# Attention in front of a mixture of experts: Q is loaded into 64 partitions instead of twice into 128

## The chip, the cores and the metric

The kernel runs on one core of one Trainium2 chip. The metric is the device time of one execution in microseconds (us), lower is better. Five engines work side by side, each on its own instruction queue: TensorE (PE, its weight loads are listed apart as PEld), VectorE (DVE), ScalarE (ACT), GpSimd (POOL) and SyncE (SP), which here only issues DMAs. A DMA is issued by a queue and then carried out by the core's 16 DMA engines. SBUF is the on-chip memory with 128 partitions; PSUM is what TensorE writes to.

## What is computed

Three layers follow each other. Only the first is touched by the change.

```python
# 1. attention: 4 batches x 8 heads, S = 576 rows, head size 64
scores = scale * np.matmul(q, k.transpose(0, 1, 3, 2))
s_pos = np.maximum(s, 0.0)
cum = np.cumsum(s_pos, axis=-1)
bias = -(cum[:, :, :, None] - cum[:, :, None, :])
scores = np.where(causal, -1000000000.0, scores + np.minimum(bias, 0.0))
attn = softmax(scores)             # max, exp, sum, divide
x = np.matmul(attn, v)             # then rows of 8 heads side by side: 2304 x 512
# 2. experts: 8 experts of 288 tokens each, tokens assigned greedily by logit
h = np.maximum(x[mask] @ w1[e], 0.0); out[mask] = h @ w2[e]
# 3. a dense layer: relu(x @ w_in) squared, @ w_out
```

## The kernel before

All matrix products are made in a 4-byte matmul type, `fp32r`. To keep full precision a float32 operand is split in two: a high part (the operand rounded to `fp32r`) and a low part (the operand less its high part). A product of two such operands then takes the terms high·high, low·high and high·low.

The attention uses the head size of 64 for this. For a head, `Q1` holds in its partitions 0 to 63 the high part of Q (transposed, so that the head dimension lies on the partitions) and in its partitions 64 to 127 the low part. `K1` holds the high part of K in both halves. One matmul of `Q1` with `K1` over all 128 partitions therefore gives high·high + low·high. `Q2` holds the high part of Q again (64 partitions) and four rows for the bias, `K2` the low part of K and four rows for the bias; a second matmul of `Q2` with `K2` over 68 partitions gives the rest.

The 32 heads are worked in 16 pairs. `load_pair(p)` loads Q and K of a pair from HBM into `q2` and `k2`, each of 128 partitions and 2 heads of 576 columns, by two DMAs each: the same 64 rows go to partitions 0 to 63 and again to 64 to 127. `prep(head, u)` makes the parts of a head. For every pair but the first, u = 0 rounds `q2` into `Q1` on DVE (L179) and copies the high part from `Q1` to `Q2` by a DMA on SP's queue (L180); u = 1 rounds `k2` into `K1` on DVE (L182), and POOL subtracts twice: K's low part into `K2` (L183) and Q's low part into the upper half of `Q1` (L184). For the first pair ACT rounds Q (L160) and writes `Q2` (L161), and DVE makes Q's low part (L177).

Each head has five score tiles, i = 4 down to 0. Each tile goes through two matmuls (L225 and L226), a mask, a row maximum on DVE (L248), an exponential on ACT (L260), transposes on TensorE (L282), copies out of PSUM on DVE or ACT, and products with V (L312). The tile i = 0 of the two heads of a pair is one tile: its two matmuls (L210) read `Q1` and then `Q2` of both heads, and they stand among the tiles of the pair's first head. The order is written out by hand: the program counts tiles, ten to a pair, and at tile numbers given by `PR` and `PR0` calls `prep` for the heads of the next pair, at tile 5 of each pair `load_pair` for the pair after that. So the second head of a pair is prepared at tile 9 of the pair before, and its `Q2` is read at tile 4 of its own pair.

SP issues nearly all DMAs in program order: the copy of the first head's `Q2`, the loads of K and Q, in most pairs one or two blocks of the third layer's weights (L912, `r<-in_wout`, 512 KB each), the copy of the second head's `Q2`, the loads of V and four or five small copies of bias rows.

After attention come the assignment of tokens to experts, the experts, and the dense layer; TensorE carries these.

Of the kernel before, what the change touches and what calls it, by code (L numbers as in the profile page):

```python
# [6 lines left out]
FT = mybir.dt.float32  # L7
# [4 lines left out]
AF = mybir.ActivationFunctionType  # L12
OP = mybir.AluOpType
# [3 lines left out]
B, H, S, D = 4, 8, 576, 64  # L17
# [16 lines left out]
def f32(ap):  # L34
    return ap.bitcast(FT)
# [33 lines left out]
def attention(tc, cn, qT, kT, vm, vt, s, wg, xd, L):  # L69
    nc = tc.nc  # L70
# [3 lines left out]
    def pool(name, bufs, **kw):  # L74
        p = tc.tile_pool(name=name, bufs=bufs, **kw)
        pools.append(p)
        return p.__enter__()
# [6 lines left out]
    ld = pool("a_ld", 2)  # L84
# [7 lines left out]
    RAW = {}  # L92

    def load_pair(p):
        q2 = ld.tile([128, 2, S], FT, name="q2")
        k2 = ld.tile([128, 2, S], FT, name="k2")
        if p == 0:
            todo = ((nc.scalar, q2, qT, 0, 1), (nc.sync, k2, kT, 0, 1), (nc.sync, k2, kT, 1, 2),
                    (nc.sync, q2, qT, 1, 2))
        else:  # L100
            todo = ((nc.sync, k2, kT, 0, 2), (nc.sync, q2, qT, 0, 2))
        for eng, t, src, a0, a1 in todo:
            if p == 1 and t is q2:
                bias(1)

            h = src[:, 2 * p + a0:2 * p + a1, :]
            for r in (0, 64):
                eng.dma_start(t[r:r + 64, a0:a1], h)
        RAW[p] = (q2, k2)

# [5 lines left out]
    def load_v(p):  # L116
# [4 lines left out]
        VB[p] = t  # L121

    load_pair(0)
    QB = fx.tile([128, 2, S], FR, name="QB")
    Q2S = [QB[0:68], fx.tile([68, 2, S], FR, name="Q21")]
    K2S = [fx.tile([68, 2, S], FR, name=f"K2{k}") for k in range(2)]

    def ones(k):
        for n, t in enumerate((Q2S[k], K2S[k])):
            nc.scalar.activation(t[64:68], cn.one[64:68, n:n + 1, None].to_broadcast([4, 2, S]), AF.Copy)  # L130
# [10 lines left out]
    PREP = {}  # L141

    def bias(hd):
        p, a = hd // 2, hd % 2
        r = f32(brow[hd:hd + 1])
        nc.sync.dma_start(f32(K2S[p % 2][66:68, a]), r)
        t = f32(Q2S[p % 2][64:66, a])
        if a:
            nc.sync.dma_start(t, r)
        else:  # L150

            nc.sync.dma_start(t[:, :S - 64], r[:, :, 64:])
            nc.sync.dma_start(t[:, S - 64:], r[:, :, :64])

    def prep0():
        q2 = RAW[0][0]
        PREP[0] = (wk.tile([128, 2, S], FR, name="Q1"), wk.tile([128, 2, S], FR, name="K1"), Q2S[0], K2S[0])
        bias(0)
        for a in range(2):
            nc.scalar.activation(PREP[0][0][:, a], q2[:, a], AF.Copy)  # L160
            nc.scalar.activation(Q2S[0][0:64, a], q2[0:64, a], AF.Copy)  # L161
        ones(1)
        prep(0, 0)

    def prep(hd, u):
        p, a = hd // 2, hd % 2
        q2, k2 = RAW[p]
        if p not in PREP:
            PREP[p] = (wk.tile([128, 2, S], FR, name="Q1"), wk.tile([128, 2, S], FR, name="K1"), Q2S[p % 2],
                       K2S[p % 2])  # L170
        Q1, K1, Q2, K2 = (t[:, a] for t in PREP[p])
        q, k = q2[:, a], k2[:, a]
        if u == 0:
            if p == 0:
                nc.vector.tensor_copy(K1, k)
                (nc.gpsimd if a else nc.vector).tensor_tensor(K2[0:64], k[0:64], f32(K1[0:64]), op=OP.subtract)
                nc.vector.tensor_tensor(Q1[64:128], q[64:128], f32(Q1[64:128]), op=OP.subtract)  # L177
                return
            nc.vector.tensor_copy(Q1, q)  # L179
            nc.sync.dma_start(f32(Q2[0:64]), f32(Q1[0:64]))  # L180
        else:
            nc.vector.tensor_copy(K1, k)  # L182
            nc.gpsimd.tensor_tensor(K2[0:64], k[0:64], f32(K1[0:64]), op=OP.subtract)  # L183
            nc.gpsimd.tensor_tensor(Q1[64:128], q[64:128], f32(Q1[64:128]), op=OP.subtract)  # L184
            if a:
                RAW.pop(p)

# [218 lines left out]
    def run_jobs(n):  # L406
        for _ in range(n):
            if jobs:
                f, a = jobs.popleft()
                f(*a)  # L410

    prep0()
    for k in range(2):
        nc.vector.memset(sums[k], 1.0)
    load_pair(1)
    load_v(0)
    cn.late_consts(0)
# [26 lines left out]
    AVO = [1, 8]  # L444
    at(2, tri_of_two)
    at(A1, prep, 1, 0)
    at(A1, RAW.pop, 0)
    at(26, gate_weights)
    for n in range(4):
        at(15 + n, cn.late_consts, 1 + n)  # L450
    for p in range(NP):
        t0 = 10 * (p + 1) + LA
        last = p == NP - 1
        avs, avo = (LS_, LO_) if last else (AVS, AVO)
        for n in range(7):
            at(t0 + avs[n], av, p, n)
        at(t0 + avo[0], av_out, p, 0)
        at(t0 + avo[1], av_out, p, 1)
        if p + 1 < NP:
            for a in range(2):  # L460
                at(10 * p + 1, bias, 2 * p + 2 + a)
                for u in range(2):
                    at(10 * p + (PR if p else PR0)[2 * a + u], prep, 2 * p + 2 + a, u)
        if p + 2 < NP:
            at(10 * p + 5, load_pair, p + 2)
        for f, n in zip((cn.conv.load, cn.conv.begin, cn.conv.begin1, cn.conv.begin2, cn.conv.end),
                        (CS0, CS1)[p] if p < 2 else CS):
            at(10 * p + n, f, *([True] if f == cn.conv.begin else []))
        if p % 4 == 3:
            b = p // 4  # L470
            t1 = t0 + (LT if last else GB[0])
            for n, (f, *a) in enumerate([(rinv, b), (gate, b, 1), (gate, b, 0)] + [(xrows_late, XA[0])] * last
                                        + [(gate2, b, *c) for c in (G2L if last else G2)] + [(xrows_late, XA[1])] * last
                                        + [(xrows, b, ii) for ii in range(5)]):
                at(t1 + n * (GB[1] if b < B - 1 else 1), f, *a)
            if b == B - 2:
                for n, (f, *a) in enumerate([(cn.front.keys, 0, 15), (cn.front.best, 0, 15),
                                             (cn.front.first, 0, 15)]):
                    at(t1 + max(18, 4 * GB[1] + 2) + 2 * n, f, *a)
# [1058 lines left out]
```

## Time and profile before

| | |
|---|---|
| time, median of 3 runs | 902.96 us (900.46 to 903.33) |
| the profiled execution: its time | 902.39 us |
| the profiled execution: its span, first to last instruction | 900.4 us |
| TensorE busy | 853.1 us, 95% of the span |
| VectorE busy | 576.6 us, 64% |
| ScalarE busy | 463.9 us, 52% |
| GpSimd busy | 276.5 us, 31% |
| DMA traffic | 96.05 MB, of it 38.82 MB in the first 200 us |

The span is what the trace covers; 2.0 us of the execution's time lie outside it. Times in the trace count from the start of the span. The attention fills about the first 200 us. An engine's busy share says how full it is over the whole kernel, not whether it sets the end: that is read from what each engine waited for.

### The profile page before, as it was taken

What the parts mean: (1) busy time and instruction counts of PE and PEld (TensorE: products, weight loads), DVE (VectorE), ACT (ScalarE), POOL (GpSimd) and SP (SyncE); (2) the same over time, 40 slices, a digit from 0 to 9 for tenths busy, and PEclk for the clock granted to TensorE, in tenths of its full rate; (3) what the DMA queues carried; (4) which work ended last, traced back from release to release, by engine and by line L of the source; (5) the groups of instructions that cost most, each with busy time, mean ns of one, the idle gap of its engine ahead of it and who ended that gap; (6) DMA issues with size and microseconds to landing.
All of it is one profiled execution on the core that took longest, in us unless ns stands there. A gap on an engine that the chain in (4) does not pass through costs nothing.

```text
span 900.4 us, 16420 instructions
## 1 busy us (share of the span) xinstructions
PE 853.1 (95%) x5728; PEld 722.6 (80%) x5728; DVE 576.6 (64%) x1606; ACT 463.9 (52%) x1069; POOL 276.5 (31%) x259
## 2 busy tenths in 40 slices
PE   5899999997799899999999999999999999999996
PEld 4677777776589777888998888998888999898885
DVE  7687888887887899857767557787433354432222
ACT  7777778876236665634543334453333454543332
POOL 2555555530113455533001001201000624613323
PEclk9999999998889999999999999999999999999999
DMA  6887887834545624106531001652000530320001
GB/s 151 201 206 198 225 222 201 213 107 135 176 142 168 195 73 130 33 15 201 149 92 39 1 1 56 207 154 78 1 1 0 162 109 1 94 82 1 1 1 47
DMA packets 77282, 96.05 MB, mean 107 GB/s; under 512 B 10480, under 2 KB 55536, under 8 KB 77200
## 3 DMA queue, kind: packets, MB, share of 16 engines
q1 hardware_dynamic: 73152, 83.18, 33.6%
q0 software_dynamic: 3360, 11.01, 3.6%
q8 instruction: 45, 0.74, 0.4%
q10 hardware_dynamic: 688, 0.82, 0.3%
q14 instruction: 37, 0.30, 0.1%
HBM read 80.83 MB, written 9.44 MB: 100 GB/s over the span
## 4 chain that ended last, share of the span: by engine, by line
PE 71%; DVE 11%; DMA 9%; issue 3%; ACT 3%; POOL 1%; SPq 1%; DVEq 0%; ACTq 0%; POOLq 0%
PE h L1154 9%; PE h L1155 9%; PE h L1156 9%; PE acc L1202 7%; PE acc L1203 7%; PE acc L1204 7%; DMA raw<-in_w 4%; PE pt L282 4%; PE av L312 3%; PE acc L1154 2%; PE acc L1156 2%; PE acc L1155 2%; DVE wL L1081 2%; PE sc L225 2%; PE sc L226 2%
## 5 line engine op out<-in xcount | busy, mean ns | idle before, releaser
L1264 ACT ACTIVATE s<-h 128x512 f32<-128x512 f32 (+1 forms) x80 | 44.3, 554 | 192.0 <-PE h L1156 173.5
L1268 DVE TENSOR_TENSOR s<-s 128x512 f32<-128x512 f32 (+1 forms) x80 | 51.0, 638 | 143.7 <-ACT sH L1267 143.5
L1154 PE MATMUL h<-yH,winH 128*128 128x512 f32 (+1 forms) x332 | 122.7, 369 | 0.0
L1155 PE MATMUL h<-yL,winH 128*128 128x512 f32 (+1 forms) x332 | 120.5, 363 | 0.0
L1156 PE MATMUL h<-yH,winL 128*128 128x512 f32 (+1 forms) x332 | 120.5, 363 | 0.0
L1078 ACT ACTIVATE wH<-raw 128x512 fp32r<-128x512 f32 x128 | 79.8, 628 | 71.1 <-DMA raw<-in_w 42.0
L1202 PE MATMUL acc<-wH,sH 128*128 128x512 f32 x288 | 114.3, 397 | 0.0
L1203 PE MATMUL acc<-wL,sH 128*128 128x512 f32 x288 | 112.5, 390 | 0.0
L1204 PE MATMUL acc<-wH,sL 128*128 128x512 f32 x288 | 112.3, 390 | 0.0
L1269 POOL TENSOR_TENSOR sL<-s,sH 128x512 fp32r<-128x512 f32 (+1 forms) x48 | 68.1, 1419 | 129.7 <-DVE s L1268 127.4
L1081 DVE TENSOR_TENSOR wL<-raw,wH 128x512 fp32r<-128x512 f32 x104 | 73.7, 713 | 47.0 <-ACT wH L1078 45.6
L260 ACT ACTIVATE e<-sc,nm 128x576 f32<-128x576 f32 (+2 forms) x144 | 80.1, 556 | 36.7 <-DVE junk L248 34.2
L248 DVE TENSOR_SCALAR_CACHE_REDUCE junk<-sc 128x576 bf16<-128x576 f32 (+2 forms) x144 | 75.5, 524 | 35.5 <-PE sc L228 25.3
L1154 PE MATMUL h<-xH,wH 128*128 128x288 f32 x256 | 79.1, 309 | 2.2 <-DVE hL L1232 2.2
L1154 PE MATMUL acc<-hH,wH 128*128 128x288 f32 x256 | 79.1, 309 | 2.0 <-ACT wH L1078 2.0
L1156 PE MATMUL acc<-hH,wL 128*128 128x288 f32 x256 | 77.2, 302 | 0.5 <-DVE wL L1081 0.5
L1155 PE MATMUL acc<-hL,wH 128*128 128x288 f32 x256 | 76.8, 300 | 0.0
L1155 PE MATMUL h<-xL,wH 128*128 128x288 f32 x256 | 76.7, 300 | 0.0
L1156 PE MATMUL h<-xH,wL 128*128 128x288 f32 x256 | 76.4, 298 | 0.1
L1156 PEld LDWEIGHTS h<-yH,winL 128*128 128x128 f32 x332 | 62.3, 188 | 10.6
L1154 PEld LDWEIGHTS h<-yH,winH 128*128 128x128 f32 x332 | 62.3, 188 | 10.2
L225 PE MATMUL sc<-K,Q 128*128 128x288 f32 (+3 forms) x160 | 61.3, 389 | 9.6 <-DVE Q L177 8.3
(246 smaller groups left out, 2013.2 us busy)
## 6 DMA issues: line engine op xcount, KB each, us to landing
raw<-in_w SPq DMA_DIRECT2D x128, 256.0 KB
k<-in_kT SPq DMA_DIRECT2D x30, 288.0 KB
q<-in_qT SPq DMA_DIRECT2D x30, 288.0 KB
r<-in_wout SPq DMA_DIRECT2D x16, 512.0 KB
r<-in_win SPq DMA_DIRECT2D x15, 512.0 KB
vb<-in_vm SPq DMA_DIRECT2D x16, 256.0 KB
Q<-Q SPq DMA_DIRECT2D x16, 144.0 KB
QB<-Q SPq DMA_DIRECT2D x14, 144.0 KB
```

The lines of the kernel that those rows point to most:

```text
L225: nc.tensor.matmul(o, Q1[:, a, q0:q0 + 128], K1[:, a, x0:x1], start=True, stop=False)
L248: nc.vector.tensor_scalar(o, v, -0.125, None, op0=OP.mult, op1=OP.min, accum_out=nm[:m])
L260: nc.scalar.activation(o, v, AF.Exp, bias=nm[:m], scale=0.125, accum_out=sums[b % 2][:m, i, hd % H:hd % H + 1] if i else both[b % 2][:, p: ...
L1078: S.activation(hi, src, AF.Copy)
L1081: (G if eng[1] == "G" else V).tensor_tensor(lo, src, f32(hi), op=OP.subtract)
L1154: T.matmul(o, wh, xh, start=first, stop=False)
L1155: T.matmul(o, wh, xl, start=False, stop=False)
L1156: T.matmul(o, wl, xh, start=False, stop=last)
L1202: T.matmul(o, hi[:, c0:c0 + 128], wh, start=f == 0, stop=False)
L1203: T.matmul(o, hi[:, c0:c0 + 128], wl, start=False, stop=False)
L1204: T.matmul(o, lo[:, c0:c0 + 128], wh, start=False, stop=f == NB2 - 1)
L1269: (V if CHUNKS[c][0] in QUIET else G).tensor_tensor(lo, s, f32(hi), op=OP.subtract)
```

## The change

`q2` becomes a tile of 64 partitions, and the second of its two load DMAs is left out, in every pair. The rounding of Q writes only the lower half of `Q1`, and the subtraction that makes Q's low part reads `q2` and the high part in partitions 0 to 63 and writes partitions 64 to 127; before, all its operands lay in 64 to 127. K is loaded to both halves as before.

```diff
-        q2 = ld.tile([128, 2, S], FT, name="q2")
+        q2 = ld.tile([64, 2, S], FT, name="q2")
         k2 = ld.tile([128, 2, S], FT, name="k2")
...
-            for r in (0, 64):
+            for r in (0, 64) if t is k2 else (0,):
                 eng.dma_start(t[r:r + 64, a0:a1], h)
...
-            nc.scalar.activation(PREP[0][0][:, a], q2[:, a], AF.Copy)
-            nc.scalar.activation(Q2S[0][0:64, a], q2[0:64, a], AF.Copy)
+            nc.scalar.activation(PREP[0][0][0:64, a], q2[:, a], AF.Copy)
+            nc.scalar.activation(Q2S[0][0:64, a], q2[:, a], AF.Copy)
...
-                nc.vector.tensor_tensor(Q1[64:128], q[64:128], f32(Q1[64:128]), op=OP.subtract)
+                nc.vector.tensor_tensor(Q1[64:128], q, f32(Q1[0:64]), op=OP.subtract)
...
-            nc.vector.tensor_copy(Q1, q)
+            nc.vector.tensor_copy(Q1[0:64], q)
             nc.sync.dma_start(f32(Q2[0:64]), f32(Q1[0:64]))
...
-            nc.gpsimd.tensor_tensor(Q1[64:128], q[64:128], f32(Q1[64:128]), op=OP.subtract)
+            nc.gpsimd.tensor_tensor(Q1[64:128], q, f32(Q1[0:64]), op=OP.subtract)
```

No instruction changes its place on any engine. On SP's queue, the third pair's loads before the change stood as follows (`k`, `q` are the loads of K and Q, `r` a block of weights, `QB<-Q` the copy into `Q2`, `vb` V; the number after a name is a buffer's):

```order
29 L180 DMA QB<-Q_448 64x576
30 L108 DMA k_473<-in_kT 64x1152 x2
31 L108 DMA q_472<-in_qT 64x1152 x2
32 L912 DMA r_490<-in_wout 128x1024
33 L180 DMA QB<-Q_448 64x576
34 L912 DMA r_536<-in_wout 128x1024
35 L119 DMA vb_158<-in_vm 128x2x256
36 L120 DMA vb_158<-in_vt 128x2x64
```

In the changed kernel the same stretch of SP's queue reads:

```order
29 L180 DMA QB<-Q_444 64x576
30 L108 DMA k_469<-in_kT 64x1152 x2
31 L108 DMA q_468<-in_qT 64x1152
32 L912 DMA r_485<-in_wout 128x1024
33 L180 DMA QB<-Q_444 64x576
34 L912 DMA r_531<-in_wout 128x1024
35 L119 DMA vb_158<-in_vm 128x2x256
36 L120 DMA vb_158<-in_vt 128x2x64
```

One of the two Q loads is gone, ahead of the second copy into `Q2`; all else stands where it stood.

## Rows read from the trace of the kernel before

**Rows 1.** The page: TensorE's busy time, and DMA share in 40 slices of the span.
```profile
PE 853.1 (95%) x5728; PEld 722.6 (80%) x5728; DVE 576.6 (64%) x1606; ACT 463.9 (52%) x1069; POOL 276.5 (31%) x259
...
DMA  6887887834545624106531001652000530320001
```

**Rows 2.** Busy time by stretch: start:end, length, five engines, PEclk, DMA share, GB/s.
```profile
20.00:60.00 40.00, 35.98 (x290) 27.65 (x291) 29.02 (x96) 31.14 (x92) 24.51 (x22) 1.00 0.87 209
60.00:100.00 40.00, 39.20 (x332) 29.82 (x331) 32.62 (x109) 31.64 (x95) 21.85 (x17) 1.00 0.78 205
...
200.00:260.00 60.00, 47.22 (x453) 37.81 (x453) 46.62 (x193) 27.47 (x96) 4.21 (x4) 0.86 0.45 139
```

**Rows 3.** What TensorE's matmuls waited for, 16 to 200 us: total, times, longest.
```profile
PE sc L210 <- issue: 2.3, 2, 1.2
PE sc L210 <- DMA QB<-Q: 1.4, 2, 0.8
PE sc L225 <- ACT e L260: 1.2, 3, 0.9
PE sc L210 <- DMA Q<-Q: 1.1, 2, 0.8
```

**Rows 4.** Timeline, TensorE: tile i = 0 of the fourth and eleventh pair.
```profile
50.79 0.36 PE L210 MATMUL sc<-K,Q 128*128 128x256 f32 x1
51.99 0.36 PE L210 MATMUL sc<-K,Q 68*128 68x256 f32 x1 [0.83 <-DMA Q<-Q]
...
136.14 0.36 PE L210 MATMUL sc<-K,Q 128*128 128x256 f32 x1
```

**Rows 5.** Timeline of SP's queue for the fourth pair.
```profile
42.60 1.78 SPq L108 DMA_DIRECT2D k<-in_kT  x2
44.48 1.19 SPq L108 DMA_DIRECT2D q<-in_qT  x2
...
47.61 0.53 SPq L180 DMA_DIRECT2D Q<-Q  x1
```

**Rows 6.** Busy time (columns as in rows 2) in stretches that end at a wait.
```profile
21.00:28.00 7.00, 5.79 (x46) 4.63 (x47) 4.05 (x14) 5.99 (x18) 3.91 (x3) 1.00 1.00 226
...
44.00:53.00 9.00, 8.17 (x73) 6.52 (x69) 7.32 (x24) 7.50 (x22) 5.22 (x4) 1.00 0.98 238
57.00:64.00 7.00, 6.41 (x58) 5.23 (x58) 5.66 (x17) 6.06 (x17) 3.56 (x3) 1.00 1.02 256
105.00:112.00 7.00, 6.24 (x57) 5.07 (x56) 6.49 (x17) 5.55 (x16) 2.83 (x2) 1.00 1.02 273
```

**Rows 7.** The page's DMA issues: count and size of each.
```profile
q<-in_qT SPq DMA_DIRECT2D x30, 288.0 KB
...
Q<-Q SPq DMA_DIRECT2D x16, 144.0 KB
```

**Rows 8.** Timeline, GpSimd: Q's low part, second head of fourth and eleventh pair.
```profile
49.13 1.41 POOL L184 TENSOR_TENSOR Q<-q,Q 64x576 fp32r<-64x576 f32 x1
...
133.28 1.41 POOL L184 TENSOR_TENSOR Q<-q,Q 64x576 fp32r<-64x576 f32 x1
```

**Rows 9.** Single lines of the program: count, shortest/median/longest ns, first and last start.
```profile
L184 POOL TENSOR_TENSOR Q<-q,Q x30: 1397/1406/1414, 20.7 to 191.0; 64x576 fp32r<-64x576 f32 x30
...
L176 POOL TENSOR_TENSOR K<-k,K x1: 1972/1972/1972, 12.0 to 12.0; 64x576 fp32r<-64x576 f32 x1
...
L329 DVE COPY sums<-both x8: 155/160/166, 75.6 to 205.7; 64x4 f32<-64x4 f32 x8
...
L160 ACT ACTIVATE Q<-q x2: 683/683/683, 6.0 to 8.2; 128x576 fp32r<-128x576 f32 x2
...
L161 ACT ACTIVATE QB<-q x2: 666/666/667, 6.6 to 8.8; 64x576 fp32r<-64x576 f32 x2
```

**Rows 10.** Timeline of the start: ACT and TensorE.
```profile
8.16 0.68 ACT L160 ACTIVATE Q<-q 128x576 fp32r<-128x576 f32 x1 [0.93 <-DMA q<-in_qT]
...
12.55 1.11 PE L282 MATMUL pt<-ident,e 128*128 128x128 f32 x4 [0.87 <-ACT e L260]
```

## The prediction

> **What bounds the kernel now.** I read the page first: TensorE is busy 853.1 of 900.4 us, so time is won only where TensorE stands idle or where something delays its start, and the DMA engines are well filled in the first nine of the 40 slices, which is the attention [rows 1]. The change lies in that stretch alone, so the busy times by stretch came next: TensorE is idle 4.0 us between 20 and 60, where the DMA share is 0.87, and only 0.8 us between 60 and 100 at a share of 0.78 [rows 2]. The view of who waited for whom then tells what those idle times are: from 16 to 200 us six of TensorE's waits, 2.3 + 1.4 + 1.1 = 4.8 us together, stand before L210, and all the rest of any length is 1.2 us of waiting for an exponential [rows 3]. Two of the six carry the label "issue" and four a DMA into `Q2`. The timeline shows which of the two matmuls of L210 it is: the first one, which reads `Q1`, starts at 50.79 without a wait, the second one, which reads `Q2`, 0.83 us late at 51.99 [rows 4]. So the copy of the second head's high part into `Q2` is what TensorE waits for. The two waits labelled "issue" stand before the same second matmul, in the second and third pair; I count them with the others.
>
> The reader should see why that copy is late. SP issues it at 47.61, behind two K loads and two Q loads issued from 42.60 on [rows 5], and it is needed at about 51.2, when the first L210 is through. In the stretches that end at such a wait the DMA engines are full: shares of 0.98 to 1.02, at 226 to 273 GB/s [rows 6]. The copy waits in a full queue of loads, a quarter or less of which is the second half of Q.
>
> **What is removed, and what it is worth.** Per pair one Q load of 288 KB goes, in 15 pairs [rows 7], and in the first pair two of 144 KB: 15 x 0.295 + 2 x 0.147 = 4.7 MB of the 38.8 MB that move in the first 200 us, and 17 issues, of about 0.59 us each (1.19 for two) [rows 5]. Each removed load stands directly ahead of the late copy. At the rates of the full stretches, 0.295 MB take 1.30 us (226 GB/s) to 1.08 us (273 GB/s) [rows 6]. The six waits are 0.2 to 1.2 us long [rows 3], and the longest ones lie in the stretch with the lowest rate, so each is covered whole or nearly so. I take 4.6 of the 4.8 us, leaving 0.2 for the longest, which the cut just reaches. What is late next is the first L210 itself: it already runs without a wait, behind transposes on TensorE, so TensorE is the bound there as it is in the pairs that have no such wait.
>
> The row gives 226 to 273 GB/s for these loads [rows 6]. The Trainium skill, DMA: Bandwidth & Descriptors, section "Where 436 GB/s comes from", puts the ceiling at 435 GB/s; by it, as an estimate, a removed load would give back only 0.68 us, and 3.6 us of the six waits would go instead of 4.6. The trace does not agree with that rate here, and the measured one decides.
>
> **At the start** ACT stands idle 0.93 us until the second head's Q has landed at 8.16, and TensorE later waits 0.87 us for ACT's first exponential [rows 10]. One Q load of 144 KB fewer is queued on SP ahead of the last one, and one on ACT's queue. The issue saved alone is about 0.6 us, so ACT can start up to 0.9 us earlier, if all of its wait goes. How much of it reaches TensorE the trace of before does not show, since VectorE, which makes the maxima for the exponentials, is itself nearly without a gap then. The bounds are 0 and 0.9 us; I take 0.4, near the middle, because only some of the tiles there wait for ACT.
>
> **Edits costed at nothing.** The rounding over 64 partitions instead of 128: ACT takes 683 ns for 128x576 and 666 ns for 64x576 [rows 9], so an instruction's width in partitions is worth 17 ns at most; VectorE's casts of Q stay in place and are off the path. The two subtractions on VectorE in the first pair that now read one half and write the other: L329 copies half of its eight times from the upper 64 partitions to the lower ones and half not, and all lie within 155 to 166 ns [rows 9], so a shift costs VectorE nothing. No order changes on any engine, and no wait is added: the subtraction on GpSimd follows another that already waits for the later cast.
>
> **The one unknown price** is the 30 subtractions on GpSimd, which read partitions 0 to 63 and write 64 to 127 now. No row of GpSimd has such a shift. Below, nothing speaks for a gain: same elements, same engine, 1.41 us [rows 9]. Above, the nearest row is the same operation without a shift at its dearest, 1.97 us at the start (L176), 0.56 more. What covers them: for the second head of a pair the subtraction ends at 49.13 + 1.41 = 50.54 and the first L210 starts at 50.79, 0.25 us of cover; in the widest case it ends at 134.69 and L210 starts at 136.14, 1.45 us [rows 4, 8]. Over the fifteen pairs the cover is 13.2 us in all, 0.9 in the mean. At 0.56 more only three pairs would lose something, 0.5 us together. I take nothing, since VectorE's shift, the nearest case, costs nothing, and keep 0.5 for the range.
>
> The sum: 902.4 (the profiled execution, span 900.4 and 2.0 outside) - 4.6 - 0.4 = 897.4 us. That execution lies 0.6 below the median of the three runs, 902.96, so against the median it is -0.6%.
>
> **Rivals.** *The gain is given back behind the attention.* From 200 to 260 the granted clock is 0.86 in the mean, so TensorE falls to its lower level of 1.2 GHz at times, and it is idle 12.8 of 60 us [rows 2]. An attention that ends 5 us earlier meets that stretch at another moment. Against it: nothing there is tied to a fixed time, all follows the end of the attention through data. The price is bounded by how far runs of one and the same program lie apart, 903.33 - 900.46 = 2.9 us; then 900.3, no change that can be told. About 0.3% (2.7 us) is what a measurement of this kernel can tell from none.
>
> *The copy is late by itself*, not for the queue: its own trip from SBUF to SBUF takes 4.4 us from issue to use [rows 4, 5], and the freed DMA time goes to weights and V. Then only the start gains, 902.0. Against it: the full DMA shares right up to the wait [rows 6], and that the other nine pairs have no wait at all with the same copy.
>
> *The shifted subtraction is slow on GpSimd*, the case on the other side. If crossing halves made it take twice its time, 2.8 us, twelve of the fifteen second heads would run out of cover: 12 x 1.41 - 8.9 = 8.0 us lost before the first L210, and the time would be 902.4 - 5.0 + 8.0 = 905.4. It decides from about 1.15 us more per subtraction (some 2.55 us each), where the loss reaches 5.0. For it speaks that the cover is thin, 0.25 us at the least; against it, that no row of this engine for this form is above 1.97 us. The Trainium skill, GPSIMD Engine Reference, section "Extended-addressing connectivity", says that for `tensor_tensor` each of this engine's cores works on its own 16 partitions, which would put reader and writer of the shifted form on different cores; it gives no price, and no run here shows one yet.
>
> *More than the sum:* the whole 0.9 us at the start and the 1.2 us of waits for exponentials go too: 902.4 - 4.8 - 0.9 - 1.2 = 895.5.
>
> **How the numbers follow.** My sum, with its neighbours from 895.5 to 900.2: 0.67. More than that: 0.05. Given back, or the copy late by itself, 900.3 to 902.5 or a little above: 0.20. The slow subtraction or another loss: 0.08. Faster by over 0.3% (below 900.25) is then 0.72, within 0.3% 0.20, slower 0.08. The predicted time is that of the likeliest case. The range goes from 894.8, the fourth rival with another 0.7 for the spread of runs, to 902.3, which takes in both cases of no change and leaves out the slow subtraction; the likeliest case alone has 895.5 to 900.2.
>
> **What the profile after would show.** Right: 15 Q loads of 288 KB instead of 30; the DMA share from 20 to 60 down from 0.87 to under 0.8; no wait of over 0.3 us before the second L210 matmul; the attention's last score tiles about 5 us earlier; L184 at 1.4 us. Wrong, if L184 takes over 2 us or TensorE waits for it before the first L210; if the copy into `Q2` still ends a wait at a DMA share well below 1; or if the attention ends 5 us earlier and the stretch behind it grows by as much.

## The result, and the profile after

The changed kernel takes 894.49 us (median of 4 runs, 891.87 to 895.18) against 902.75 us before (4 runs); the ratio is 0.9913, with a 95% interval of 0.9886 to 0.9941. It is faster by 8.3 us, 0.9%. The forecast was 897.4 us, 5.4 us under this median of before; the measured time lies 0.3 us below the low end of the range, which is less than the interval of the ratio (some 2.5 us to either side). The direction and the place were right, the size was too small.

The page of the changed kernel, engines and DMA share in 40 slices, answers to [rows 1]:

```profile
PE 850.1 (95%) x5728; PEld 718.4 (81%) x5728; DVE 576.2 (65%) x1606; ACT 463.8 (52%) x1069; POOL 276.9 (31%) x259
...
DMA  5777777625556424017421003552000630320001
```

The first eight slices stand at 5 to 7 tenths where they stood at 6 to 8. The busy times by stretch, as in [rows 2]:

```profile
20.00:60.00 40.00, 39.49 (x321) 30.42 (x322) 31.95 (x102) 33.35 (x99) 25.44 (x22) 1.00 0.80 198
60.00:100.00 40.00, 39.80 (x334) 29.59 (x332) 32.56 (x109) 31.66 (x95) 23.47 (x18) 1.00 0.67 173
...
200.00:260.00 60.00, 48.05 (x457) 39.81 (x456) 51.07 (x210) 26.92 (x93) 7.21 (x7) 0.89 0.53 163
```

TensorE's idle time between 20 and 60 fell from 4.0 to 0.5 us. What TensorE's matmuls waited for from 15 to 195 us, as in [rows 3]:

```profile
PE sc L225 <- ACT e L260: 1.2, 3, 0.9
PE pt L282 <- ACT e L260: 0.5, 1, 0.5
PE pt L278 <- ACT e L260: 0.5, 1, 0.5
PE sc L210 <- DMA QB<-Q: 0.5, 2, 0.3
PE sc L210 <- DMA Q<-Q: 0.4, 1, 0.4
```

The waits before L210 went from six and 4.8 us to three and 0.9 us. In the fourth pair the two L210 matmuls now follow each other, merged into one row, and the copy into `Q2` is issued at 44.54, behind one Q load instead of two (two small loads, `wbd`, of 8 KB each stand between them in both kernels); compare [rows 4] and [rows 5]. First TensorE, then SP's queue:

```profile
48.07 0.53 PE L210 MATMUL sc<-K,Q 128*128 128x256 f32 x2
```

```profile
39.99 2.10 SPq L108 DMA_DIRECT2D k<-in_kT  x2
42.18 0.55 SPq L108 DMA_DIRECT2D q<-in_qT  x1
...
44.54 0.53 SPq L180 DMA_DIRECT2D Q<-Q  x1
```

The second of the two matmuls, which reads `Q2`, starts 0.2 us into that row, at about 48.2: that is 3.7 us from the copy's issue to its use, instead of 4.4. The page's DMA issues show 15 Q loads for 30 [rows 7]:

```profile
q<-in_qT SPq DMA_DIRECT2D x15, 288.0 KB
```

The subtraction on GpSimd that now crosses halves takes what it took, and ACT's rounding over half the partitions too [rows 9]:

```profile
L184 POOL TENSOR_TENSOR Q<-q,Q x30: 1401/1408/1415, 19.7 to 185.3; 64x576 fp32r<-64x576 f32 x30
...
L160 ACT ACTIVATE Q<-q x2: 682/682/682, 4.9 to 6.8; 64x576 fp32r<-64x576 f32 x2
```

At the start ACT has both heads' Q earlier: the second head's rounding starts at 6.78 instead of 8.16 [rows 10], the first head's at 4.86 instead of 5.98, the first exponential at 10.72 instead of 11.66.

```profile
4.86 0.68 ACT L160 ACTIVATE Q<-q 64x576 fp32r<-64x576 f32 x1
6.78 0.68 ACT L160 ACTIVATE Q<-q 64x576 fp32r<-64x576 f32 x1 [0.66 <-DMA q<-in_qT]
10.72 0.74 ACT L260 ACTIVATE e<-sc,nm 128x576 f32<-128x576 f32 x1 [0.46 <-DVE junk L248]
```

The score matmuls of the last head start at 188.28 instead of 193.96. Before, then after:

```profile
193.96 0.38 PE L225 MATMUL sc<-K,Q 128*128 128x288 f32 x1
```

```profile
188.28 0.38 PE L225 MATMUL sc<-K,Q 128*128 128x288 f32 x1
```

So 5.7 us of the gain between these two profiles are made in the attention, and the other 2.3 of the 8.0 us in span lie behind it.

Of the signs that the prediction named, the Q loads, the time of L184 and the end of the attention came out. Two were missed by little: the DMA share from 20 to 60 is 0.80 and not under it, and two waits before the second L210 are over 0.3 us, 0.32 in the third pair and 0.37 in the fourteenth. The last one also touches a sign of being wrong, a copy that ends a wait at a DMA share well below 1: in the 7 us before it the share is 0.84. First that stretch (columns as in [rows 2]), then the matmul that waits:

```profile
157.10:164.10 7.00, 6.63 (x61) 5.52 (x59) 5.65 (x17) 6.10 (x19) 4.55 (x4) 1.00 0.84 221
```

```profile
164.10 0.36 PE L210 MATMUL sc<-K,Q 68*128 68x256 f32 x1 [0.37 <-DMA Q<-Q]
```

That copy takes 4.5 us from issue to use in both kernels (159.59 to 164.10, before 165.27 to 169.74). In this pair and this profile the removed load did not help; in the two later profiles of the changed kernel no wait is listed there.

The experiments had to say whether the queue is what was freed, what the start is worth, and where the 2.3 us come from.

### The profile page after: what moved, and what is told of

It reads as the page before. It is cut to its first block, busy times and chain, and to the rows that moved or that the text cites. A ratio compares the mean times of both kernels' runs of the same rounds, so it can differ in the third digit from the quotient of the medians.

```text
span 892.4 us, 16395 instructions
## 1 busy us (share of the span) xinstructions
PE 850.1 (95%) x5728; PEld 718.4 (81%) x5728; DVE 576.2 (65%) x1606; ACT 463.8 (52%) x1069; POOL 276.9 (31%) x259
## 2 busy tenths in 40 slices
DMA packets 75922, 91.33 MB, mean 102 GB/s; under 512 B 10208, under 2 KB 55264, under 8 KB 75840
## 4 chain that ended last, share of the span: by engine, by line
PE 60%; DVE 9%; DMA 5%; issue 3%; ACT 2%; POOL 2%; SPq 0%; DVEq 0%; ACTq 0%; POOLq 0%
PE h L1154 9%; PE h L1156 9%; PE h L1155 9%; PE acc L1202 7%; PE acc L1203 7%; PE acc L1204 7%; DMA raw<-in_w 3%; PE acc L1154 3%; PE acc L1155 2%; PE acc L1156 2%; DVE wL L1081 2%; PE mi L1121 1%; ACT wH L1078 1%; PE mi L749 1%; POOL wL L1081 1%
## 5 line engine op out<-in xcount | busy, mean ns | idle before, releaser
L1155 PEld LDWEIGHTS h<-yL,winH 128*128 128x128 f32 x332 | 62.4, 188 | 10.0
```

What stands on the lines that cost most here:

```text
L1155: T.matmul(o, wh, xl, start=False, stop=False)
```

## The experiments

In each of the comparisons below the runs of the kernel before were made on the same chip.

**Both halves loaded, all else changed.** Edit against the changed kernel; the upper half of `q2` is loaded and not read:

```diff
-        q2 = ld.tile([64, 2, S], FT, name="q2")
+        q2 = ld.tile([128, 2, S], FT, name="q2")
...
-            for r in (0, 64) if t is k2 else (0,):
+            for r in (0, 64):
...
-        q, k = q2[:, a], k2[:, a]
+        q, k = q2[0:64, a], k2[:, a]
```

> The changed arithmetic (narrow rounding, shifted subtraction), but Q is still loaded to both halves; the upper half is not read. Theory (the removed load freed the queue ahead of the late copy into Q2): the six waits before the second L210 come back, the attention ends where it did before, time within 1 us of before, 902 us. Rival (part of the gain comes from the narrower instructions or the shifted subtraction): 1 to 3 us faster than before.

Measured: ratio to before 1.0013 (0.9994 to 1.0031), 903.92 us. The whole gain is gone, and the waits before L210 are back, 1.8 + 1.6 + 0.8 + 0.7 = 4.9 us:

```profile
PE sc L210 <- DMA Q<-Q: 1.8, 2, 1.3
PE sc L210 <- DMA r<-in_wout: 1.6, 1, 1.6
...
PE sc L210 <- issue: 0.8, 1, 0.8
PE sc L210 <- DMA QB<-Q: 0.7, 1, 0.7
```

The narrow rounding and the shifted subtractions give nothing, and cost nothing that the interval can tell (it reaches up to 0.3%); the gain is the load's.

**The second half loaded behind the copy.** Edit against the changed kernel (with `q2` of 128 partitions, as above):

```diff
             nc.sync.dma_start(f32(Q2[0:64]), f32(Q1[0:64]))
+            if a and p + 1 in RAW:
+                nc.sync.dma_start(RAW[p + 1][0][64:128], qT[:, 2 * p + 2:2 * p + 4, :])
```

> The changed kernel, with the second half of Q loaded again, unread, for 14 pairs, but issued behind the second copy into Q2 instead of ahead of it. Theory (only what stands ahead of the copy in the queue counts): the bytes are back and the gain stays, waits before the second L210 under 1.5 us in all, 894 to 896 us. Rival (the traffic as a whole is what counts): 899 to 902 us.

Measured: ratio 0.9914 (0.9897 to 0.9931), 895.21 us, the changed kernel's time with 14 of the 15 loads back. On SP's queue the fourth pair reads:

```profile
38.89 2.05 SPq L108 DMA_DIRECT2D k<-in_kT  x2
41.03 0.56 SPq L108 DMA_DIRECT2D q<-in_qT  x1
...
43.36 0.52 SPq L180 DMA_DIRECT2D Q<-Q  x1
43.92 0.60 SPq L182 DMA_DIRECT2D q<-in_qT  x1
```

One wait of 0.7 us is left in this list before the tile i = 0 (L212 in this kernel):

```profile
PE sc L212 <- DMA QB<-Q: 0.7, 1, 0.7
```

This settles the first question. Neither the traffic (95.46 MB here, 91.33 in the changed kernel) nor the number of issues made a difference that can be told; what counts is what stands ahead of the copy in the queue. The first pair's second half and the second pair's stayed out in this kernel, so the start is that of the changed kernel.

**Only the first pair loaded once, and all but the first.** The loop of the first experiment with another condition, first with only the first pair loaded once, then with all but the first:

```diff
-            for r in (0, 64):
+            for r in (0, 64) if t is k2 or p else (0,):
...
-            for r in (0, 64):
+            for r in (0, 64) if t is k2 or not p else (0,):
```

> The changed arithmetic; only the first pair's Q is loaded once, all other pairs to both halves. Theory: only the start gains, TensorE 0.8 to 1.0 us earlier from the second head on, the six waits come back: 901.5 us. Rival (the start matters more, since later waits shrink when the loads begin earlier): 899 to 900 us.

> The changed arithmetic; the first pair's Q is loaded to both halves as before, all other pairs once. Theory: the waits before the second L210 are gone and only the start (about 1 us) is missing: 895 to 896.5 us. Rival (the start carries more than 1 us): 897 us or more.

Measured: 1.0009 (0.9994 to 1.0024), 904.03 us, with the first pair alone; 0.9909 (0.9894 to 0.9925), 895.32 us, with all the others. The profiles show the start plainly: the second pair's first score matmul starts at 20.40 with the first pair loaded once and at 21.39 with it loaded twice. In the times it is not to be seen in either kernel. For the first, both expectations were missed, the theory's 901.5 us and the rival's 899 to 900: the interval reaches down to 0.5 us of gain at most. The second lies in the theory's 895 to 896.5 us, but not for the theory's reason: its ratio is that of the changed kernel, so the start that is missing does not show as a loss. In the profile with the first pair loaded once the last head stands at 192.37, 1.6 us before that of the kernel before, with 699.1 us behind it, 1.0 us more; that execution, 901.84 us, was the second shortest of its twelve. Where the rest of the start's gain goes is not shown.

**The changed kernel again, and the kernel before again**, unedited, for more profiles.

> The changed kernel once more, to see a second profile of it. Theory (the 2.3 us of gain behind the attention come from where TensorE's clock falls, which differs between executions): the attention ends within 0.2 us of the first profile, and the stretch behind it differs from the first profile by 1 us or more, or the clock rows differ. Rival (they follow from the earlier end of the attention by data alone): the same stretch within 0.3 us.

> The changed kernel for a third profile. Theory: waits before the second L210 of under 1 us in all, the last head at 186 to 188.5 us, the stretch behind it 704 to 707 us long. Rival (it is always shorter than that of the kernel before): 704 to 705 us.

> The kernel before, for a second profile of it. Theory (the waits before the second L210 are what the attention loses, the rest of the difference behind the attention is spread between executions): six or so waits of 4 to 6 us in all, the last head at 192 to 194 us, and the stretch behind it within the spread of the others, 704 to 708 us long. Rival (the stretch behind the attention is longer by 2 us in the kernel before, in every execution): 706 us or more.

Measured: the changed kernel 0.9911 (0.9893 to 0.9929), 894.76 us, and in a single run 893.32; the kernel before 902.57 in a single run. In the two new profiles of the changed kernel the last head starts at 186.50 and 187.13; the expected 0.2 us from the first profile's 188.28 were missed, since the three attentions differ by up to 1.8 us. 1.0 of it is there by the start of the second pair (20.18 and 20.19 against 21.17), in the rest the L210 waits went to none and to 0.6 us. The second profile of the kernel before has its last head at 194.03, with 4.8 us of waits before L210.

From the starts of the last head's and of the very last matmul each profile gives the length of the stretch behind the attention. Worked out so, it is 698.0 and 698.1 us in the two profiles of before, 699.4 with both halves loaded, 699.1 with the first pair loaded once; and 695.7, 696.3 and 695.8 in the three of the changed kernel, 696.6 with the load behind the copy, 695.9 with all but the first pair once. The means are 698.7 and 696.1.

The expectations count this stretch to the end of the span. So counted it is 706.5 us in the second profile of before, and 704.1, 704.7 and 704.2 in the three of the changed kernel. 706.5 and 704.2 fit both the theory and the rival of their expectations. The first two of the changed kernel lie 0.6 us apart, more than the rival's 0.3 and less than the theory's 1; their clock rows differ, 0.94 against 0.95 from 195 to 335, which the theory allowed.

My theory that this part is only spread between executions does not fit: the two groups do not overlap. The rival in the expectations fits better, and the load behind the copy shows that it does not hang on the bytes loaded.

Two of the five long ones are long partly for another reason. With both halves loaded, and with the first pair loaded once, TensorE's clock falls once more at 574 to 576 us, among the experts, after TensorE stood idle 1.97 and 1.73 us for VectorE. With both halves loaded (columns as in [rows 2]), then the kernel before:

```profile
574.00:581.00 7.00, 5.17 (x27) 5.17 (x28) 5.02 (x15) 2.73 (x6) 0.00 (x0) 0.76 0.42 122
```

```profile
574.00:581.00 7.00, 7.00 (x62) 6.93 (x62) 5.79 (x18) 3.23 (x6) 0.00 (x0) 1.00 0.45 124
```

Up to the dense layer's first product into `acc` (`acc<-wH,sH`) the stretch takes 124.8 and 124.4 us in the kernel before, 123.2 with both halves loaded and 123.0 with the first pair once, against 122.1, 122.0 and 122.5 in the changed kernel, 122.8 with the load behind and 121.6 with all but the first pair once. The groups still do not overlap, but only 0.2 us lies between their nearest members. Between the kernel before and the changed kernel alone the whole stretch differs by 2.2 us (698.1 against 695.9), and all of it arises in these first 125 us.

**The start delayed.** Unread loads ahead of the first K loads, 256 KB each, into the three buffers of V (`VF`); three of them in the changed kernel, six in the changed kernel (`VF + VF`, the last three wait for the first three), and three in the kernel before:

```diff
+    for t in VF:
+        nc.sync.dma_start(t[:, :, 0:4, :], vm[0, :, 0:2])
     load_pair(0)
```

> The changed kernel with three unread loads of 256 KB put ahead of the first K loads, so that all starts 3 to 4 us later. Theory (what follows the attention follows it by data): the changed kernel's time plus that delay, 898 to 899 us. Rival (the 2.3 us behind the attention depend on the moment at which it ends): 900 us or more.

> The changed kernel with six unread loads ahead of the first K loads (three of them wait for the three before), so that its attention ends about where that of the kernel before does. Theory (the stretch behind the attention follows by data; how long TensorE runs at 1.2 GHz in it is not set by the moment): from the last head to the last matmul 694.5 to 697 us, as in the six profiles with Q loaded once. Rival (the moment at which the attention ends sets the clock behind it): 698 to 699.5 us, as in the four profiles with Q loaded twice, and a mean clock of 0.984 or less.

> The kernel before with three unread loads of 256 KB ahead of the first K loads. Theory: the waits before the second L210 stay, the time is that of the kernel before plus 3 to 4 us, 906 to 907 us, and the stretch from the last head to the last matmul 698 us or more. Rival (a later start shrinks the waits, or the moment of the attention's end sets the clock): 904 us or less, or that stretch under 697 us.

Measured: 0.9946 (0.9929 to 0.9963), 898.16 us, with three; 0.999 (0.9971 to 1.0009), 902.53 us, with six; 1.0042 (1.0027 to 1.0058), 905.99 us, for the kernel before with three. The first matmul starts 3.1 us later with three (11.27 against 8.16), 5.5 us later with six (13.63). Three loads cost 0.9946 - 0.9911 = 0.35%, 3.1 us, what they delay, and 898 to 899 us was expected. Six cost 0.79%, 7.1 us, 1.6 more than they delay the first matmul, and 1.1 more than they delay the last head (193.31, against 187.3 in the mean of the three profiles without delay). The kernel before with three keeps 4.9 us of waits, and its 905.99 us lie at the low end of the theory's 906 to 907. In the kernel delayed by six the last head stands nearly where it stands in the kernel before, though its attention has hardly a wait left. First its last head, then its last matmul (the lines have moved by two):

```profile
193.31 0.38 PE L227 MATMUL sc<-K,Q 128*128 128x288 f32 x1
...
891.82 0.39 PE L1206 MATMUL acc<-wH,sL 128*128 128x512 f32 x1
```

In the changed kernel's second profile:

```profile
186.50 0.38 PE L225 MATMUL sc<-K,Q 128*128 128x288 f32 x1
...
882.78 0.39 PE L1204 MATMUL acc<-wH,sL 128*128 128x512 f32 x1
```

891.82 - 193.31 = 698.5 us, against 882.78 - 186.50 = 696.3. In this profile the changed kernel with its attention moved to the old moment has the old length behind it, as the rival said. Each side is one execution, though: the delayed one, 902.21 us, lies in the middle of its twelve, 899.42 to 904.75, while the second profile of the changed kernel, 893.18 us, was the shortest of its six. With three loads, the last head at 190.34, the stretch is 694.6 us; that execution too, 895.36 us at a mean clock of 0.990, was the shortest of its six by 2.5 us, and the others have 0.980 to 0.985. The kernel before, delayed by three, has its last head at 197.85 and 697.2 us behind it, neither the 698 of the theory nor quite the under 697 of its rival. Put in order of the moment: 694.6 to 696.6 for last heads from 186.5 to 190.3, 698.0 to 699.4 from 192.4 to 194.0, 697.2 at 197.9.

What differs most in that stretch is TensorE's clock. The stretch from 195 to 335 in four kernels (columns as in [rows 2]). The kernel before:

```profile
195.00:335.00 140.00, 121.30 (x971) 104.42 (x970) 112.16 (x354) 75.95 (x192) 36.31 (x28) 0.91 0.47 144
```

The changed kernel, second profile:

```profile
195.00:335.00 140.00, 121.56 (x969) 103.69 (x966) 116.23 (x352) 76.29 (x184) 42.32 (x32) 0.95 0.48 149
```

The changed kernel delayed by six loads:

```profile
195.00:335.00 140.00, 121.17 (x966) 104.18 (x967) 113.25 (x351) 77.02 (x194) 37.15 (x28) 0.91 0.45 143
```

The changed kernel with the load behind the copy:

```profile
195.00:335.00 140.00, 121.56 (x962) 104.40 (x961) 114.51 (x347) 74.99 (x183) 40.04 (x30) 0.91 0.47 146
```

Over all twelve profiles the mean granted clock of these 140 us is 0.91 to 0.93 where the stretch behind the attention is 697.2 us or longer and 0.94 or 0.95 where it is shorter, that is, TensorE runs at 1.2 GHz instead of 2.4 for more of the time in the long ones. The one exception is the last row, 0.91 with a short stretch, so the clock alone does not tell the two groups apart. TensorE is idle part of the time where these falls lie: from 200 to 260 it is busy 47 to 48 of 60 us in both kernels. Over all runs the mean clock of the whole span is 0.984 for the kernel before (57 runs) and 0.988 for the changed one (11 runs). Among the 57 runs a straight line gives 4.7 us less for each 0.010 more of clock. By that, as an estimate, the clock goes with 1.5 us of the difference between the kernels (their mean clocks lie 0.0032 apart); that the clock is the cause is not shown by it.

## Why the prediction was right in place and short in size

*The bound.* The late copy into `Q2` behind the loads was the wait that ends last in the attention. This is shown by the load put back ahead of the copy (gain gone) and behind it (gain kept). The rival that the copy is late by itself is out as the main cause: with one load fewer ahead of it the copy arrives in time in all but three pairs. For the fourteenth pair it may hold, where the first profile has 0.37 us of wait and the copy's trip is unchanged at 4.5 us. "Directly ahead of the late copy" was not exact: in the third pair a block of weights, 512 KB, stands between the Q loads and the copy.

*The term of the waits, 4.6 us,* was nearly right. From the first score matmul of the second pair to that of the last head the two profiles of before and the one with both halves loaded take 171.8, 172.1 and 172.4 us; the three of the changed kernel and the one with the load behind take 167.1, 166.3, 166.9 and 167.3. The difference of the means is 5.2 us. It is more than the waits that went, which fell from 4.8, 4.8 and 4.9 us to 0.9, 0, 0.6 and 0.7, by 4.3 in the mean; where the other 0.9 us come from is not shown.

*The rate.* The rows' 226 to 273 GB/s fit what a load ahead of the copy costs: the longest waits of 1.2 us went down to 0.4 or less. The 0.68 us per load that followed from the ceiling in the Trainium skill, DMA: Bandwidth & Descriptors, section "Where 436 GB/s comes from", would have left 1.2 us of waits; the changed kernel's profiles have 0.9, 0 and 0.6. The difference is small beside the spread of the profiles, and the row's rate fits better. The ceiling itself is not contradicted, since the measured rate lies below it.

*The term of the start, 0.4 us with bounds 0 and 0.9,* was too small, its upper bound too. The second pair begins at 22.14, 21.92, 21.29 and 21.39 with the first pair loaded twice and at 21.17, 20.18, 20.19, 20.17 and 20.40 with it loaded once: 1.3 us between the means. Before, then after:

```profile
22.14 0.40 PE L225 MATMUL sc<-K,Q 128*128 128x288 f32 x1
```

```profile
21.17 0.40 PE L225 MATMUL sc<-K,Q 128*128 128x288 f32 x1
```

The step that failed is the bound: I took ACT's one wait of 0.93 us [rows 10] as all there was to win, but the first head's Q comes earlier as well, 4.86 against 5.98, so ACT's whole row of work moves up by more than that wait. The trace of before already had a wait there that I left out (the second profile of before does not have it, and starts this rounding at 5.51):

```profile
5.98 0.68 ACT L160 ACTIVATE Q<-q 128x576 fp32r<-128x576 f32 x1 [0.50 <-DMA q<-in_qT]
```

This term is read from profiles only: in the times of the two kernels that differ in the first pair it is not to be seen.

*The edits costed at nothing* cost nothing: 1408 ns against 1406 for the subtraction on GpSimd that crosses from partitions 0 to 63 into 64 to 127. The rival on the other side did not come true. The Trainium skill, GPSIMD Engine Reference, section "Extended-addressing connectivity", has each core work on its own 16 partitions for `tensor_tensor`; whatever the cores do here, a shift by 64 partitions has no price in the trace.

*What lies behind the attention* is where the sum fell short most. "Nothing there is tied to a fixed time, all follows the end of the attention through data" does not fit the profiles: I priced the stretch's clock only as a rival that gives gain back, by up to 2.9 us, and in the profiles the stretch gave 2 to 3 us on top instead. The price was short too: it came from three runs, and the 57 runs of the kernel before, on three chips, lie up to 8.4 us apart. That the attention's earlier end is met by a shorter stretch stands in all profiles without a delay; that the moment is the cause rests on one profile of the kernel delayed to the old moment. The times of that kernel agree (1.6 us more than its delay) but by themselves do not settle it, with intervals of 0.16 to 0.19%, about 1.5 us, to either side. Why the moment matters, and whether it recurs at other moments, stays open; the one point beyond, at 197.9, lies between the two groups.

Together: 1.3 + 5.2 + 2.2 (698.1 - 695.9, the kernel before and the changed kernel alone) = 8.7 us by the means of the profiles, 8.3 us by the medians of the times. By the times alone the last term is not clear of nothing: the ratio of 0.9911 is 8.0 us with 6.4 to 9.7, which leaves 1.5 us, -0.1 to 3.2, beside the 6.5 of the attention.

## What to carry to other kernels

Where a short transfer on the critical path is issued behind bulk loads, cost each load ahead of it at the measured rate of the full stretch; here a load moved behind it was worth as much as a load removed. Duplicating data by a second load was dearer here than an engine operation that reads one half of the partitions and writes the other, since the transfer queue was full and that engine had to write the other half anyway. A gain in one stage need not arrive unchanged at the end: here a later stage in which TensorE's clock rises and falls seems to have added to it. So delay the changed kernel on purpose before giving the rest a cause, and take several profiles of each, since one execution can be 2 to 3 us off its median.

## What the runs showed of the hardware that was not expected

In one profile each, the changed kernel delayed by some 6 us has a stretch behind its attention that is 2.2 us longer (698.5 against 696.3), with the same work there and the same order; whether it does so in every execution is not shown. And the start of one program differs between executions by 1 us: the second pair of the changed kernel began at 21.17, 20.18 and 20.19 in three profiles, with ACT's first exponential at 10.72 or 10.73 in all three.
